# An order of work for 30 attention chunks: both score sets side by side, both transposes together, and routing in six parts

## The chip, the cores and the metric

The kernel runs on one core of one Trainium2 chip. The metric is the device time of one execution in microseconds (us), the median of several runs. Engines: TensorE (PE; PEld are its weight loads), VectorE (DVE), ScalarE (ACT), GpSimd (POOL), and SyncE (SP), which only issues DMAs.

## The reference

Sliding-window attention, and then a mixture of experts with one expert for each token:

```
scores = q @ k.T / 8 - slope_h * |i - j|     where 0 <= i - j < 128, else -1e9
attn   = softmax(scores);   x = (attn @ v), heads side by side   # 8 batches, 8 heads, 576 tokens, 64 wide
logits = x @ w_gate;        e = argmax(logits);   g = softmax(logits)[e]
out    = g * (relu(x @ w1[e]) @ w2[e])       # 4608 tokens, 512 wide, 8 experts, 1024 hidden
```

All inputs and the output are fp32.

## The kernel before, in words

The 4608 tokens are 36 chunks of 128 query rows. For a pair of batches there are nine chunks: four of the first batch, a "tail" chunk with the last 64 rows of both batches, and four of the second. The first chunk of a batch (m = 0) has no keys before it: its value products are 16 matmuls instead of 32, and nothing has to be masked. In a tail chunk they are 64 smaller ones. With chunk 0 first, the m = 0 chunks are 0, 5, 9, 14, 18, 23, 27 and 32, and the tail chunks 4, 13, 22 and 31.

A chunk goes through these operations, each of which exists for two sets of four heads (set 0 and set 1) where a digit follows the letter:

- S0, S1 (`scores`, lines 158 to 187; TensorE): 8 bf16 matmuls write the bias into a set's PSUM banks (L173), then 32 fp32 matmuls add q times k (L182), in array tiles of 64x32. There is one pair of banks for each set, so S0 of the next chunk needs the exponentials of set 0 of this chunk to be over, and S1 those of set 1.
- F0, F1 (`fold`; VectorE): a predicated copy puts the window's two halves into one (L192, left out for m = 0), and a maximum is taken (L195).
- E0a, E0b, E1a, E1b (`exps`; ScalarE): two heads each, exponential and sum (L224).
- T0, T1 (`turn`; TensorE): four 128x128 transposes into a PSUM bank (L232). C0, C1 (ScalarE) copy them into `pT` (L336). P0a to P1b (`select`; GpSimd) mask them (L247). Z (GpSimd) adds an epsilon to the sums.
- A0, A1 (`av`; TensorE): the value products (L263), in tiles of 128x64 into another bank of the same two-buffer pool that T0 and T1 use. X (ScalarE) copies them to `xT` (L345).
- R (`rows`; TensorE): 8 matmuls (128x128) turn `xT` back to rows and add the gate logits (L271), into the only buffer of `r_ps`. I, L, Y (VectorE): reciprocal of the sums, scaled logits and scaled rows (L276). Y also issues the DMA of the rows to memory on SP (L1308).

What stands where is written out by hand. Each operation has a time in chunks (the table `WHEN`, from line 402): operation "op" of chunk ch is issued at ch + WHEN[op], all operations are sorted by that, and each engine works through its own in that order. So in the table below T0=1.02 puts the first transposes of chunk ch just behind the first scores of chunk ch + 1:

```
WHEN = {None: dict(
    S0=0, F0=0.06, S1=0.063, E0a=0.332, E0b=0.407, F1=0.604, E1a=0.611, E1b=1.002, T0=1.02, C0=1.03,
    P0a=1.04, T1=1.043, P0b=1.282, C1=1.376, P1a=1.472, P1b=1.516, Z=1.753, A0=2.75, A1=2.76, X=2.963,
    I=3.06, R=4.027, L=4.119, Y=4.237)}
```

A quarter of a chunk is a step (`step`, line 355). Behind the operations of a step come the loads that fall due, the parts of `route` (L526 to L595: VectorE and a few bf16 matmuls that give each token its rank in its expert; a generator that runs to its next `yield` at every fourth step), and halves of the first expert's weights, which ScalarE rounds (`round_half`, L1078) and GpSimd subtracts (`rest_half`, L1083). Groups of five or six chunks are routed together (`GROUPS`); three late groups have steps of their own (`PACE`).

After the 36 chunks the order by hand ends (step 152), and the expert layers follow: TensorE multiplies in three passes of split precision (L767, L973), with rows gathered and scattered by GpSimd's indirect DMAs.

Of the kernel before, what the change touches and what calls it, by code (L numbers as in the profile page):

```python
# [36 lines left out]
def attention(ctx, tc, st, qT, qE, kT, v, c1, cb, iw, load_c2, logits, chunk_done, chunks, begun):  # L37
# [320 lines left out]
    def step(s):  # L358
        st["step"] = s
        if s == 0:  # L360
            begun(0)
        if s == 12:
            begun(1)
        for f in opening.get(s, ()):
            f()
        for f, b, m in ahead.get(s, ()):
            f(b, m)
        while plan and plan[0][0] < (s + 1) / 4 - 1e-6:
            _, _, op, ch = plan.pop(0)
            do(op, ch)  # L370
        if s < len(WU) - 1:
            warm_up(WU[s + 1])
        for k in list(st["stages"]):
            if k[1] <= s and (s in PACE[k[2]] if k[2] in PACE else s % 4 == STAGE):
                k[1] = s + 1
                if next(k[0], k) is k:
                    st["stages"].remove(k)
        n, i = divmod(s - FETCH, 8)
        for k in range(2):
            if 0 <= n < 7 and i == ROUND + 4 * k:  # L380
                st["round"](n, k)
            if 0 <= n - (REST + 4 * k) // 8 < 7 and i == (REST + 4 * k) % 8:
                st["rest_of"](n - (REST + 4 * k) // 8, k)
        n, i = divmod(s - FETCH + 12, 8)
        for k in range(2):
            if 0 <= n < 8 and i == LOAD + 4 * k:
                st["load"](n, k)
        if s in EP:
            early(EP[s])
        if s == HAND - 1:  # L390
            st["last"]()
# [6 lines left out]
    s = HAND  # L398
# [6 lines left out]
# [3 lines that stand above are left out]
# [1 line left out]
WHEN[1] = dict(T1=1.55, C1=1.56, P1a=1.57, P1b=1.58, U=1.61, Z=1.9)  # L409
WHEN[2] = dict(T1=1.057, C1=1.56, P1a=1.57, P1b=1.58, U=1.61, Z=1.9)  # L410
APIECE = (0, 1, 2)
WHEN[4] = dict(A0=2.26)
WHEN[13] = dict(A0=2.26)
WHEN[22] = dict(A0=2.26)
WHEN[31] = dict(A0=2.26)
WHEN[33] = dict(X=2.77, I=3.75, R=3.76, L=3.77, Y=3.78)
WHEN[34] = dict(A0=2.51, A1=2.52, X=2.53, I=3.25, R=3.26, L=3.27, Y=3.28)
WHEN[35] = dict(
    T0=1.02, C0=1.03, E1a=1.053, E1b=1.054, Z=1.055, T1=1.262, C1=1.31, P1a=1.32, P1b=1.456, A0=2.01,
    A1=2.02, X=2.03, I=2.55, R=2.56, L=2.57, Y=2.58)  # L420
STAGE = 3
ROUND = 0
REST = 7
# [13 lines left out]
FETCH = 57  # L437
# [80 lines left out]


def route(tc, st, lg, c0, G, groups):  # L520
    nc = tc.nc
    rp = st["rp"]
    run = st["run"]
# [26 lines left out]
        nc.tensor.matmul(out=rank[:, E * g:], lhsT=tri[:, 1, :], rhs=f2(oh[:, 0:G - g]), start=False, stop=g == G - 1)  # L550
    pick = rp.tile(sh3, F32, name="pick")
    nc.vector.tensor_tensor(out=pick, in0=rank.rearrange("p (g e) -> p g e", e=E), in1=oh, op=ALU.mult)
    gate = rp.tile([128, G], F32, name="gate")
    nc.vector.tensor_reduce(out=gate, in_=ex, axis=AX.X, op=ALU.add)
    put_gates(tc, st, gate, groups)
# [68 lines left out]
def route_last(tc, st, lg, ch, groups):  # L624
    nc = tc.nc
    rp = st["rp"]
    run = st["run"]
    tri = st["tri"]
    prev = rp.tile([128, E], BF16, name="l_prev", bufs=1)
    nc.vector.tensor_copy(out=prev, in_=run[:, ch, :])  # L630
    mx = rp.tile([128, 2], F32, name="l_mx", bufs=1)
    nc.vector.tensor_reduce(out=mx[:, 0:1], in_=lg, axis=AX.X, op=ALU.max)
    key = rp.tile([128, E], F32, name="l_key", bufs=1)
    nc.vector.scalar_tensor_tensor(out=key, in0=lg, scalar=mx[:, 0:1], in1=st["rev"], op0=ALU.is_ge, op1=ALU.mult)
    nc.vector.tensor_scalar(out=mx[:, 1:2], in0=mx[:, 0:1], scalar1=-1.0, scalar2=None, op0=ALU.mult)
    mk = st["mk"][:, ch:ch + 1]
    nc.vector.tensor_reduce(out=mk, in_=key, axis=AX.X, op=ALU.max)
    ex = rp.tile([128, E], F32, name="l_ex", bufs=1)
    gate = rp.tile([128, 1], F32, name="l_gate", bufs=1)
    nc.scalar.activation(out=ex, in_=lg, func=AF.Exp, bias=mx[:, 1:2], accum_out=gate)  # L640
    oh = rp.tile([128, E], BF16, name="l_oh", bufs=1)
    nc.vector.tensor_scalar(out=oh, in0=key, scalar1=mk, scalar2=None, op0=ALU.is_equal)
    rest = [r for r, *_ in st["stages"]]
    st["stages"].clear()
    st["warm"](0)
    rank = st["four"]()[:, 0, 0:E]
    nc.tensor.matmul(out=rank, lhsT=tri[:, 0, :], rhs=oh, start=True, stop=False)
    nc.tensor.matmul(out=rank, lhsT=tri[:, 1, :], rhs=prev, start=False, stop=True)
    for r in rest:
        next(r)  # L650
    put_gates(tc, st, gate, groups)
    for r in rest:
        next(r)
    rr = rp.tile([128, 2, E], BF16, name="l_rr", bufs=1)
    for k, n in enumerate(("tokh", "tokl")):
        nc.vector.tensor_scalar(out=rr[:, k, :], in0=oh, scalar1=st[n][:, ch:ch + 1], scalar2=None, op0=ALU.mult)
    pick = rp.tile([128, E + 56], F32, name="l_pick", bufs=1)[:, 0:E]
    s = st["rank"][:, ch:ch + 1]
    nc.vector.tensor_tensor_reduce(out=pick, in0=rank, in1=oh, op0=ALU.mult, op1=ALU.add, scale=1.0, scalar=0.0,
                                   accum_out=s)  # L660
    t0 = EARLY // 128
    lps = {}
    for t in range(t0, TT):
        lps[t] = rp.tile([128, 128], BF16, name=f"l_lp{t}", bufs=1)
        nc.vector.tensor_scalar(out=lps[t], in0=st["i128"], scalar1=s, scalar2=-128.0 * t, op0=ALU.subtract,
                                op1=ALU.is_equal)
    st["warm"](1)
    for r in rest:
        list(r)
    ip = st["four"]()[:, 0, 0:E * TT]  # L670
    for t, lp in lps.items():
        for k in range(2):
            nc.tensor.matmul(out=ip[:, E * t:E * t + E], lhsT=lp, rhs=rr[:, k, :], start=(k == 0), stop=(k == 1))
    st["warm"](2)
    v = lambda ap: ap.rearrange("p (e t) -> p t e", t=TT)
    nc.vector.tensor_tensor(out=v(st["idx"])[:, t0:], in0=v(st["base"])[:, t0:],
                            in1=ip.rearrange("p (t e) -> p t e", e=E)[:, t0:], op=ALU.add)
    nc.vector.tensor_copy(out=v(st["idx"])[:, 0:t0], in_=v(st["base"])[:, 0:t0])
    nc.vector.tensor_tensor(out=v(st["base"])[:, t0:], in0=v(st["base"])[:, t0:],
                            in1=ip.rearrange("p (t e) -> p t e", e=E)[:, t0:], op=ALU.add)  # L680
    nc.vector.tensor_tensor(out=run[:, ch + 1, :], in0=run[:, ch, :], in1=oh, op=ALU.add)
    for low in st["parts"][1:]:
        low()


# [91 lines left out]
def moe_early(ctx, tc, st):  # L777
# [8 lines left out]
    h = {}  # L786
    w = {}
    parts = []
    st["parts"] = parts

    def step(op, bank):
        if op == "z":
# [478 lines left out]
@with_exitstack  # L1271
def attn_moe_kernel(ctx, tc, qT, qE, kT, v, c1, cb, c2, iw, w12, out):
    nc = tc.nc
    st = {"stages": [], "w12": w12}
    moe_pools(ctx, tc, st)
    load_c2 = load_consts(tc, st, c2)
    moe_early(ctx, tc, st)
# [4 lines left out]
    with ExitStack() as actx:  # L1282
# [15 lines left out]
        def done(ch, subs, x_sb):  # L1298
            c0, G = next((c, n) for c, n in GROUPS if c <= ch < c + n)
            if ch == c0 + G - 1:  # L1300
                lg = lgp.tile([128, 8, E], F32, name="lg")[:, 0:G, :]
                nc.vector.tensor_reduce(out=lg, in_=lgs["all"].rearrange("q g p c e -> q g e (p c)"), axis=AX.X, op=ALU.add)
            for lo in (0, 2):
                if lo == 2 and subs[0][0] == subs[2][0]:
                    continue
                n = 64 if subs[0][0] != subs[2][0] else 128
                t0 = subs[lo][0] * S + QB * subs[lo][1]
                nc.sync.dma_start(out=st["xd"][t0:t0 + n].rearrange("t (p x) -> t p x", p=NP),  # L1308
                                  in_=x_sb[QB * lo:QB * lo + n])
            if ch == c0 + G - 1:  # L1310
                groups = []
                for k in range(G):
                    sb = chunks[c0 + k]
                    t0 = sb[0][0] * S + QB * sb[0][1]
                    if sb[0][0] != sb[2][0]:
                        groups.append((k, (0, 64, t0, 1)))
                        groups.append((k, (64, 64, sb[2][0] * S + QB * sb[2][1], 1)))
                    elif groups and groups[-1][1][1] == 128 and groups[-1][1][2] + 128 * groups[-1][1][3] == t0:
                        k0, (p0, n0, s0, m0) = groups[-1]
                        groups[-1] = (k0, (p0, n0, s0, m0 + 1))  # L1320
                    else:
                        groups.append((k, (0, 128, t0, 1)))
                if ch == N // 128 - 1:
                    st["last"] = lambda: route_last(tc, st, lg[:, 0, :], ch, groups)
                else:
                    r = route(tc, st, lg, c0, G, groups)
                    st["stages"].append([r, st["step"] + (c0 not in PACE), c0])

        attention(actx, tc, st, qT, qE, kT, v, c1, cb, iw, load_c2, logits, done, chunks, begun)
    st["rc"] = ctx.enter_context(tc.tile_pool(name="rc", bufs=1))  # L1330
# [44 lines left out]
```

## Time and profile before

| | us |
|---|---|
| median of 3 runs | 645.15 (645.06 to 647.49) |
| the profiled execution's own time | 640.79 |
| its span, first to last instruction | 639.1 |
| TensorE busy | 626.4 |
| VectorE busy | 385.2 |
| ScalarE busy | 315.4 |
| GpSimd busy | 295.0 |

An engine's busy time is what its instructions cover together. Matmuls overlap each other and their ends are modelled, so the distance from one group's start to the next group's start says more than their durations. A row of a timeline has the start, the time from first start to last end of a merged group, engine, line and operation, what is written and read, the tile in the array for matmuls, the shape, the count, and in brackets the idle time of the engine ahead of it with what ended it ("issue": nothing that the profile shows).

### The profile page before, as it was taken

Reading aid. Unit: us, or ns where it says so; the run is one execution under the profiler, and the core shown is the slowest. Engines: PE = TensorE matmul, PEld = TensorE weight load, DVE = VectorE, ACT = ScalarE, POOL = GpSimd, SP = SyncE. Lnnn points to the kernel's source line nnn. Section 1 sums busy time; section 2 is a strip of 40 time slices with the busy share of each in tenths; the row PEclk is TensorE's granted clock in tenths of the full one; section 3 lists DMA queues with packets and bytes.
Section 4 is the critical chain, followed back from the end, with each engine's and each line's share of the span. In section 5 each row is a group of like instructions: output and inputs, shape, how many; then the busy total and the mean of one; then the engine's idle time right before and its main releaser. Section 6 shows DMA issues by size and latency. Waiting matters only on the chain.

```text
span 639.1 us, 17958 instructions
## 1 busy us (share of the span) xinstructions
PE 626.4 (98%) x7125; PEld 540.9 (85%) x7125; DVE 385.2 (60%) x962; ACT 315.4 (49%) x939; POOL 295.0 (46%) x405
## 2 busy tenths in 40 slices
PE   8999999999999999999999999999999999999996
PEld 4778888888887988988989899899899998888884
DVE  5758877969888785536543664565465456356411
ACT  5878888888878314534342434334233333333311
POOL 3644657758646050067327606733760860580202
PEclk9999999999999999999999999999999999999998
DMA  8777887887743152474536425433543542544201
GB/s 247 218 233 190 281 246 224 233 251 214 225 131 87 51 185 70 160 251 112 187 115 169 108 75 183 121 91 127 158 108 100 172 117 88 181 120 136 68 1 61
DMA packets 60072, 97.44 MB, mean 152 GB/s; under 512 B 12293, under 2 KB 30597, under 8 KB 59986
## 3 DMA queue, kind: packets, MB, share of 16 engines
q1 hardware_dynamic: 51362, 76.25, 39.1%
q0 software_dynamic: 8336, 19.76, 11.4%
q8 instruction: 57, 0.93, 0.6%
q14 instruction: 29, 0.24, 0.1%
q10 hardware_dynamic: 288, 0.26, 0.1%
HBM read 77.27 MB, written 18.98 MB: 151 GB/s over the span
## 4 chain that ended last, share of the span: by engine, by line
PE 76%; issue 10%; DVE 6%; POOL 4%; ACT 3%; DMA 1%; POOLq 0%; ACTq 0%; DVEq 0%; SPq 0%
PE y_ps L973 25%; PE l_ps L767 25%; PE b_ps L263 7%; PE b_ps L232 4%; PE s_ps L182 4%; PE r_ps L271 4%; POOL xg L747 2%; PE s_ps L173 2%; ACT pe L224 2%; PE s_ps L767 1%; DVE s_ps L192 1%; DVE nmax L195 1%; POOL out L961 1%; DMA c_sb<-c 1%; PE x_ps L728 1%
## 5 line engine op out<-in xcount | busy, mean ns | idle before, releaser
L770 ACT ACTIVATE hh<-l_ps 128x320 fp32r<-128x320 f32 (+5 forms) x104 | 46.4, 448 | 198.2 <-PE l_ps L767 198.1
L774 DVE SCALAR_TENSOR_TENSOR hl<-l_ps,hh 128x320 fp32r<-128x320 f32 (+5 forms) x104 | 52.2, 502 | 145.6 <-ACT hh L770 145.5
L747 POOL DMA_INDIRECT xg<-xd,od_idx x112 | 116.8, 1043 | 34.5 <-issue 33.6
L224 ACT ACTIVATE pe<-s_ps,nmax 128x128 f32<-128x128 f32 x264 | 97.9, 390 | 27.2 <-DVE nmax L195 23.6
L973 PE MATMUL y_ps<-wh,hh 128*128 128x512 f32 x280 | 110.0, 393 | 0.0
L973 PE MATMUL y_ps<-wl,hh 128*128 128x512 f32 x280 | 109.5, 391 | 0.0
L973 PE MATMUL y_ps<-wh,hl 128*128 128x512 f32 x280 | 109.1, 390 | 0.0
L961 POOL DMA_INDIRECT out<-y,od_pidx x33 | 34.6, 1047 | 148.8 <-ACT y L979 142.7
L247 POOL TENSOR_SCALAR_AFFINE_SELECT pT<-pT 128x512 f32<-128x512 f32 x112 | 71.7, 648 | 59.6 <-ACT pT L336 56.4
L1066 DVE TENSOR_TENSOR wl<-w_raw,wh 128x512 fp32r<-128x512 f32 x114 | 73.8, 689 | 33.8 <-ACT wh L1062 32.2
L767 PE MATMUL l_ps<-xh,wh 128*128 128x320 f32 (+8 forms) x416 | 81.2, 317 | 0.0
L767 PE MATMUL l_ps<-xl,wh 128*128 128x320 f32 (+8 forms) x416 | 80.8, 316 | 0.0
L767 PE MATMUL l_ps<-xh,wl 128*128 128x320 f32 (+8 forms) x416 | 80.7, 316 | 0.0
L767 PEld LDWEIGHTS l_ps<-xh,wh 128*128 128x128 f32 x416 | 67.6, 188 | 6.7 <-issue 1.2
L767 PEld LDWEIGHTS l_ps<-xl,wh 128*128 128x128 f32 x416 | 66.1, 188 | 2.0
L767 PEld LDWEIGHTS l_ps<-xh,wl 128*128 128x128 f32 x416 | 65.9, 188 | 2.0
L263 PE MATMUL b_ps<-pT,v_sb 128*64 128x128 f32 (+2 forms) x1152 | 66.3, 265 | 0.8 <-issue 0.7
L263 PEld LDWEIGHTS b_ps<-pT,v_sb 128*64 128x64 f32 (+1 forms) x1152 | 57.1, 136 | 9.9 <-issue 5.2
L1062 ACT CAST wh<-w_raw 128x1024 fp32r<-128x1024 f32 x57 | 59.5, 1044 | 6.4 <-DMA w_raw<-w 6.4
L973 PEld LDWEIGHTS y_ps<-wh,hl 128*128 128x128 f32 x280 | 52.6, 188 | 11.4
L973 PEld LDWEIGHTS y_ps<-wh,hh 128*128 128x128 f32 x280 | 52.6, 188 | 9.9 <-ACT hh L770 0.4
L973 PEld LDWEIGHTS y_ps<-wl,hh 128*128 128x128 f32 x280 | 52.6, 188 | 9.2
(220 smaller groups left out, 935.1 us busy)
## 6 DMA issues: line engine op xcount, KB each, us to landing
w_raw<-w SPq DMA_DIRECT2D x56, 512.0 KB, 3.8
xd<-x_sb SPq DMA_DIRECT2D x32, 258.0 KB, 3.5
v_sb<-v SPq DMA_DIRECT2D x32, 256.0 KB, 4.6
q_sb<-qT SPq DMA_DIRECT2D x31, 256.0 KB, 4.4
k_sb<-kT SPq DMA_DIRECT2D x23, 256.0 KB, 5.4
w_raw<-w SPq DMA_DIRECT2D x16, 256.0 KB, 4.6
k_sb<-kT SPq DMA_DIRECT2D x8, 384.0 KB, 5.4
w_n<-w SPq DMA_DIRECT2D x3, 1024.0 KB, 5.4
```

What stands on the lines that cost most here:

```text
L182: nc.tensor.matmul(out=s_ps[rows(u), c, n, x0:x1], lhsT=blocks["q", b, m][h, 2 * g + n, rows(u % 2 if tail else u)], rhs=batch[b][h, 2 * g ...
L224: nc.scalar.activation(out=pe[:, h, :], in_=s_ps[:, c, n, lo:lo + 128], func=AF.Exp, bias=nmax[:, 2 * c + n:2 * c + n + 1], scale=1.0, acc ...
L247: nc.gpsimd.affine_select(out=part(cut(kb)), in_=part(cut(1)), pattern=pat(sign), base=0, channel_multiplier=-sign, compare_op=op, fill=0.0)
L263: nc.tensor.matmul(out=x_ps[64 * c:64 * c + 64, p, q], lhsT=blocks["v", b, m - 1 + kb][0:kk, D * h:D * h + D], rhs=pT[0:kk, kb, h, q], sta ...
L747: ins = tc.nc.gpsimd.indirect_dma_start(out=g[:, s], out_offset=None, in_=parts, in_offset=bass.IndirectOffsetOnAxis(ap=idx[:, s], axis=0),)
L767: nc.tensor.matmul(out=ps, lhsT=a[:, 128 * d:128 * d + 128], rhs=b[:, d], start=(k == 0), stop=(k == 11))
L770: nc.scalar.activation(out=hh, in_=ps, func=AF.Relu)
L774: nc.vector.scalar_tensor_tensor(out=hl, in0=ps, scalar=0.0, in1=hh.bitcast(F32), op0=ALU.max, op1=ALU.subtract)
L961: ins = nc.gpsimd.indirect_dma_start(**kw).ins
L973: nc.tensor.matmul(out=ys[t], lhsT=a[:, tl], rhs=b[:, 512:1024], start=(f == 0 and k == 0), stop=(f == 7 and k == 2))
L1062: keep(tc, nc.scalar.copy(out=wh, in_=raw))
L1066: keep(tc, eng.tensor_tensor(out=wl[:, sl], in0=raw[:, sl], in1=wh.bitcast(F32)[:, sl], op=ALU.subtract))
```

## The change

Chunks 5 to 34 get a table of their own. Both score sets stand at the head of a chunk, then both transposes of the chunk before, the row matmuls of the chunk three before (R at 3.41 instead of 4.027), and the value products of the chunk two before. Chunks 3 and 4 get the new times for R, I, L and Y, and chunk 4 an earlier E1b. The special A0 of tail chunks goes. Chunks 33 and 34 keep their own entries over the new table. `route` gets one more `yield` for the groups that have no steps of their own; its six parts run in turn at the third step of a chunk ("h") or, for the two with matmuls, at the fourth ("p"), at most one in a chunk. The rounding of weight halves comes one step earlier.

```diff
+        for k in list(st["parts"]):
+            if k[1] < s and s % 4 == (2, 3)[k[2][0] == "p"]:
+                k[1], k[2] = s + 1, k[2][1:]
+                if next(k[0], k) is k:
+                    st["parts"].remove(k)
+        n, i = divmod(s - FETCH + (s < 4 * SIDE[1]), 8)
         for k in range(2):
             if 0 <= n < 7 and i == ROUND + 4 * k:
                 st["round"](n, k)
+        n, i = divmod(s - FETCH, 8)
+        for k in range(2):
...
-WHEN[4] = dict(A0=2.26)
-WHEN[13] = dict(A0=2.26)
-WHEN[22] = dict(A0=2.26)
-WHEN[31] = dict(A0=2.26)
...
+SIDE = (5, 35)
+for ch in range(*SIDE):
+    WHEN[ch] = {**dict(
+        S0=0, S1=0.001, F0=0.16, T0=1.25, T1=1.33, C0=1.37, F1=0.38, R=3.41, E0a=0.46, P0a=1.5, E0b=0.55, P0b=1.6,
+        A0=2.61, I=3.62, L=3.63, Y=3.65, E1a=0.65, A1=2.75, E1b=0.8, C1=1.98, X=3.07, P1a=2.1, P1b=2.2, Z=1.3),
+        **(WHEN[ch] if ch > 32 else {})}
+for ch in (SIDE[0] - 2, SIDE[0] - 1):
+    WHEN.setdefault(ch, {}).update(R=3.41, I=3.62, L=3.63, Y=3.65)
+WHEN[SIDE[0] - 1].update(E1b=0.95)
+PARTS = "hphhhp"
...
     nc.vector.tensor_tensor(out=pick, in0=rank.rearrange("p (g e) -> p g e", e=E), in1=oh, op=ALU.mult)
+    if fine:
+        yield
     gate = rp.tile([128, G], F32, name="gate")
```

## Rows read from the trace of the kernel before

**Rows 1.** The page, part 1: busy us, share of the span and instructions of each engine.
```profile
PE 626.4 (98%) x7125; PEld 540.9 (85%) x7125; DVE 385.2 (60%) x962; ACT 315.4 (49%) x939; POOL 295.0 (46%) x405
```

**Rows 2.** Windows: length, then busy us (instructions) of each engine, clock, DMA share, GB/s.
```profile
27.52:196.28 168.76, 166.56 (x3949) 139.13 (x3948) 133.18 (x340) 141.39 (x590) 100.34 (x168) 1.00 0.75 219
...
223.00:639.00 416.00, 409.75 (x2312) 362.41 (x2309) 211.68 (x492) 142.04 (x242) 173.07 (x189) 1.00 0.42 125
```

**Rows 3.** Timeline of PE, a plain chunk (22), to the routing matmuls behind it.
```profile
122.64 0.33 PE L173 MATMUL s_ps<-cb_sb 64*32 64x320 bf16 x8
122.79 0.73 PE L182 MATMUL s_ps<-k_sb,q_sb 64*32 64x160 f32 x32
123.45 0.66 PE L232 MATMUL b_ps<-c_sb,pe 128*128 128x128 f32 x4
123.94 1.15 PE L271 MATMUL r_ps<-iw_sb,xT 128*128 128x144 f32 x8
124.92 0.60 PE L232 MATMUL b_ps<-c_sb,pe 128*128 128x128 f32 x4
125.45 0.33 PE L173 MATMUL s_ps<-cb_sb 64*32 64x320 bf16 x8
...
126.26 1.97 PE L263 MATMUL b_ps<-pT,v_sb 128*64 128x128 f32 x32
128.16 0.42 PE L593 MATMUL r_ps<-rr,lp 128*128 128x48 bf16 x10
```

**Rows 4.** Timeline of PE: routing matmuls straight before value products (chunk 31).
```profile
176.90 0.27 PE L550 MATMUL r_ps<-oh,tri 128*128 128x40 bf16 x5
177.10 1.97 PE L263 MATMUL b_ps<-pT,v_sb 128*64 128x128 f32 x32
```

**Rows 5.** Waits of PEld, 27.52 to 196.28: us in total, times, longest.
```profile
PEld b_ps L232 <- ACT pe L224: 1.3, 6, 0.2
```

**Rows 6.** Timeline of PE: groups that were held up (chunks 12, 21 and 24).
```profile
68.33 0.86 PE L232 MATMUL b_ps<-c_sb,pe 128*128 128x128 f32 x4
...
116.84 0.33 PE L173 MATMUL s_ps<-cb_sb 64*32 64x320 bf16 x8 [0.43 <-ACT pe L224]
116.97 1.04 PE L182 MATMUL s_ps<-k_sb,q_sb 64*32 64x160 f32 x32
...
139.28 1.61 PE L263 MATMUL b_ps<-pT,v_sb 64*64 64x64 f32 x38 [0.70 <-issue]
```

**Rows 7.** Timeline of ACT, chunk 22: an exponential, a copy, an exponential, a half-cast.
```profile
126.52 0.36 ACT L224 ACTIVATE pe<-s_ps,nmax 128x128 f32<-128x128 f32 x1
...
126.86 0.58 ACT L336 COPY pT<-b_ps 128x512 f32<-128x512 f32 x1
127.33 0.39 ACT L224 ACTIVATE pe<-s_ps,nmax 128x128 f32<-128x128 f32 x1
...
128.02 0.64 ACT L1078 CAST wh<-w_raw 128x512 fp32r<-128x512 f32 x1
```

**Rows 8.** Timeline of DVE: a fold, and a routing part up to the next fold.
```profile
121.02 0.70 DVE L192 COPY_PREDICATED s_ps<-c_sb,s_ps 128x512 f32<-128x512 uint32 x1 [0.38 <-PE s_ps L182]
121.75 0.69 DVE L195 TENSOR_REDUCE nmax<-s_ps 128x4 f32<-128x512 f32 x1
122.36 0.47 DVE L580 TENSOR_TENSOR c<-c,t 128x5 f32<-128x5 f32 x1
...
124.92 0.41 DVE L192 COPY_PREDICATED s_ps<-c_sb,s_ps 128x256 f32<-128x256 uint32 x1
```

**Rows 9.** Timeline, chunks 4 and 5: an exponential on ACT, the logits on DVE.
```profile
28.34 0.39 ACT L224 ACTIVATE pe<-s_ps,nmax 128x128 f32<-128x128 f32 x1
...
29.88 0.23 DVE L276 TENSOR_TENSOR lg_all<-r_ps,rinv 128x64 f32<-128x64 f32 x1 [0.70 <-PE r_ps L271]
```

**Rows 10.** Timeline of PE: transposes of chunk 35, value products of chunk 34.
```profile
204.20 1.21 PE L232 MATMUL b_ps<-c_sb,pe 128*128 128x128 f32 x4
205.34 1.97 PE L263 MATMUL b_ps<-pT,v_sb 128*64 128x128 f32 x32
```

More of the change, by code (lines that the diff above doesn't have):

```diff
@@ L377, in step @@
                     st["stages"].remove(k)
-        n, i = divmod(s - FETCH, 8)
+        for k in list(st["parts"]):
[4 more added lines that the diff above has]
+        n, i = divmod(s - FETCH + (s < 4 * SIDE[1]), 8)
         for k in range(2):
@@ L520, in route @@
 def route(tc, st, lg, c0, G, groups):
+    fine = c0 not in PACE
     nc = tc.nc
@@ L681, in route_last @@
     nc.vector.tensor_tensor(out=run[:, ch + 1, :], in0=run[:, ch, :], in1=oh, op=ALU.add)
-    for low in st["parts"][1:]:
+    for low in st["low_parts"][1:]:
         low()
@@ L788, in moe_early @@
     parts = []
-    st["parts"] = parts
+    st["low_parts"] = parts
     def step(op, bank):
@@ L1273, in attn_moe_kernel @@
     nc = tc.nc
-    st = {"stages": [], "w12": w12}
+    st = {"stages": [], "parts": [], "w12": w12}
     moe_pools(ctx, tc, st)
@@ L1326, in done @@
                     r = route(tc, st, lg, c0, G, groups)
-                    st["stages"].append([r, st["step"] + (c0 not in PACE), c0])
+                    if c0 in PACE:
+                        st["stages"].append([r, st["step"], c0])
+                    else:
+                        st["parts"].append([r, st["step"], PARTS])
         attention(actx, tc, st, qT, qE, kT, v, c1, cb, iw, load_c2, logits, done, chunks, begun)
```

## The prediction

> **What bounds the kernel now.** I read the page's busy shares first: TensorE is at 98% [rows 1]. Then the windows: the stretch from chunk 5's first score matmul (27.52) to chunk 35's (196.28) holds the 30 chunks that are reordered. It takes 168.76 us, 5.63 per chunk, with the clock granted in full; TensorE is busy for 166.56 of it, ScalarE for 141.39, VectorE for 133.18 [rows 2]. The expert stage behind it, from 223 us on, is TensorE's too, so time saved or lost ahead of it reaches the end. Third, TensorE's timeline of a plain chunk. The ends of matmuls are modelled, so I go by starts: scores to transposes 0.81, four transposes 0.49, row matmuls 0.98, four transposes and the way to the next scores 0.53, scores to value products 0.81, value products 1.90, in all 5.52 [rows 3]. So the chunk is bound by TensorE's own work and by the gaps where it changes kind; waits for other engines are the rest of the 5.63.
>
> The waits have places. The last transpose of the second set waits for the last exponential, six times [rows 5]; such a group takes 0.86 [rows 6] where a plain one takes 0.60 [rows 3]: about 0.26 each, 1.5 with one longer. In chunk 21 routing on VectorE makes the folds late: the gap ahead of the scores is 0.43 and the scores take 1.04 [rows 6] for 0.73 [rows 3], 0.8 in all. Smaller waits of this sort, read off the same timeline, add 0.8. Together 3.1 us could go. Two more gaps, "issue" inside a run of equal matmuls (0.70 in [rows 6], another at 40.3), are no wait for an engine; I keep them on both sides.
>
> **The change part by part.** *Order on TensorE.* The kinds ran scores, transposes, rows, transposes, scores, values; now scores twice, transposes twice, rows, values. The 32 score matmuls go in four waves: from first start to last end 0.73, one takes 0.30, so waves are (0.73-0.30)/3 = 0.145 apart, and a second score block can follow 0.15+0.43+0.145 = 0.73 after the first began, where transposes follow after 0.81 [rows 3]: 0.08 saved. The gap from transposes to scores (0.53 against 4 x 0.11 = 0.44) goes, but one from row matmuls to value products comes. No row shows fp32 row matmuls followed by value products. Bounds: 0.20 from start to start, as from transposes to scores, which cancels exactly; or 0.10 less, since routing's last bf16 matmul group to value products takes only 177.10-176.90 = 0.20 for all five matmuls [rows 4], which would save 3 us more over 30 chunks. I take the cancelling end, since the nearer row has fp32 operands of the same size. Sum: 30 x -0.08 = -2.4 (from -5.4 to 0).
>
> What the second gap is: when the kind changes, the weight loads of the new kind start late, and only then. The Trainium skill, TensorEngine Tiling (Array Packing), section Key Properties, says that changing the tiling mode drains the engine; by it the step from 128x128 row matmuls to 128x64 value products pays like the others, which speaks against the larger saving; the routing row by itself would allow it.
>
> *ScalarE's ring.* The second score set of the next chunk may not overwrite its banks before this chunk's last exponential. From the second scores' start: 0.81 to the transposes, 0.65 to their modelled end, about 0.1 to the copy, copy 0.47, eight exponentials of 0.35, 0.2 until the last result is in and seen [rows 3, 7]: 5.0 us. A plain chunk leaves 5.44, so 0.4 is to spare. In the seven chunks whose value products are 16 instead of 32 (7, 11, 16, 20, 25, 29, 34), TensorE wants only 5.44-0.88 = 4.56, and waits 0.45. Routing matmuls in two of these fill 0.6: 7 x 0.45 - 0.6 = +2.5 (from 0 to +4). The old waits of 3.1 go, since their place goes: the last transpose now has a whole block of scores before it.
>
> The x copy, the half-cast of weights (0.64, one step earlier) and the second pT copy run on ScalarE before the transposes end: after the last exponential there is about 1.6 us until the first pT copy can start, and the three need 0.47+0.47+0.5. Cost nothing; without that cover each would lengthen the ring by its own time.
>
> *VectorE.* Folds take 1.34 each [rows 8]; two folds, reciprocal, logits and rows end 4.9 us into a chunk, and the next fold is due at 6.5. A routing part has some 1.6 us, and late folds are hidden by another 0.2 behind the copy and the ring's 0.4. The largest part (clipped position, one-hot, two products) took 122.36 to 124.92, 2.56 [rows 8]: over by some 0.3 at worst. The first part's exponential stands between two score exponentials and waits for VectorE: 0.35 where the ring has no room, once. I take +0.4 (from 0 to +5: sixteen VectorE parts by 0.3).
>
> *GpSimd and SP.* The second set's selects now follow the copy at the next chunk's head, ahead of a weight half and the first set's selects; the value products are two thirds of a chunk behind: nothing. The row writes wait on SP in the third quarter instead of the first; behind them stand loads of v for two chunks later: nothing. Without that distance a late load would show as waiting value products.
>
> *The seam.* Chunk 4 has the old order for its copies and exponentials, chunk 5 the new one. (i) Chunk 4's last exponentials started at 28.34 [rows 9]; they move ahead of one copy (0.47) to 27.87 and end near 28.7. The second score set of chunk 5 is now due at 27.52+0.62 = 28.14: +0.6. (ii) On VectorE the logits of an older chunk (order 5.119) now stand before chunk 5's first fold (5.16). They waited for the row matmuls already [rows 9]; now the fold waits behind them, about 2 us later, exponentials end late, and chunk 6's scores wait 0.3 and 0.7: +1.0. (iii) In chunk 6 two row groups fall together (order 6.027 and 6.41) on one PSUM buffer. Logits, first fold (1.34) and rows (0.7) of the first stand between: the second starts 1.8 late, and TensorE is in order. Sum +3.4 (from +1 to +4.5). The second row group itself (0.98) is work drawn forward.
>
> *The end.* Chunk 36 has no row matmuls of chunk 32 any more (-0.98). The last transposes of chunk 35 waited before too: 1.21 for 0.60, value products at 205.34 [rows 10], 9.06 after chunk 35's first score matmul. Now a pT copy stands before its last exponentials: x copy until 6.1, copy 6.6, four exponentials 8.1, products at 8.5. So -0.6, the moved rows included.
>
> Sum: -2.4 -3.1 +2.5 +0.4 +3.4 +1.0 (rows drawn forward) -0.6 = +1.2. The profiled execution took 640.79 (span 639.1 and 1.7 around it) and would become 642.0; the median of the runs shown is 4.4 above it, so I carry the difference over: 645.15 + 1.2 = 646.3 us.
>
> **Rivals.** (1) Faster: the ring and the seam are paid from slack. For: ScalarE is idle for 16% of the stretch [rows 2] and it waited, not worked, ahead of many exponentials. Against: the order is fixed on each engine, and the seam's orders are read directly. Then -2.4 -3.1 and the end's gain: about -5, 640.0. (2) Slower: VectorE. Routing now falls in six parts between the row scaling and the next fold, a hole of 1.6 us. If VectorE reaches that hole half a microsecond later than I reckon, because the row matmuls now come behind both transposes, the fold is late in each chunk with a routing part, and the ring's room is used up: sixteen parts by 0.3 to 0.5 add 5 to 8 to my sum: about 652. It decides where parts exceed 1.6+0.6 us; for it speaks the 2.56, against it that the other parts are near 1.5. (3) The row-to-value gap is cheap, as the bf16 row: another -3, 643. (4) The order on TensorE is not what ends these chunks, other waits fill what is freed: no change, 645.
>
> **Chances.** Forecast 0.47 (its own range 643.5 to 649), rivals 0.15, 0.17, 0.10, 0.11. A measurement of this kernel can tell about 0.5%, 3.2 us, from no change. Faster: rival 1 and a third of rival 3 with its neighbours, 0.20. Slower: rival 2 and the upper edge of the forecast, 0.23. Same: 0.57. The range 640.5 to 650 leaves out part of rival 1 and most of rival 2, about 2 in 10, and holds the ends of the costs added with mixed signs.
>
> **What would show it.** Right: in the timeline after, transposes start 0.73+0.81 after the first scores; row matmuls to value products near 1.07; a plain chunk near 5.44; gaps of 0.45 before the second scores in the chunk after a 16-product one, released by an exponential; 1.8 us before the second row group of chunk 6. Wrong: no gap there (rival 1); idle TensorE before scores, released by VectorE, in the routing chunks (rival 2); 0.98 from rows to values (rival 3). A new wait on a load of v or q, or "issue" gaps inside the doubled score block, would be a cost that I have not counted.

## The result, and the profile after

Over 13 runs each the changed kernel takes 648.63 us (646.88 to 650.58), the kernel before 644.62 (642.68 to 647.49): ratio 1.0063 [1.0049, 1.0077], 4.0 us slower. The forecast was +1.2 us, 646.3 within 640.5 to 650. So the time lies inside the range, and 0.63% (0.49 to 0.77) stands at the edge of the 0.5% which can be told from no change: a little slower, where no difference was given the larger chance. Forecast and measurement differ by 2.8 us, and several terms were off in both directions; the largest single miss, 2.0 us, is the end of the attention stage.

The profiled execution of the changed kernel took 647.77, span 646.0. The new lines shift those behind line 377 (`step` stands at line 358 in both kernels, the table `WHEN` at 404 before and 411 after): the transposes and bias matmuls keep L232 and L173, the rank matmuls are L560 now, the last routing matmuls L609, the first expert layer L783.

The page after, part 1 (busy us, share of the span, instructions of each engine), to stand beside [rows 1]:

```profile
PE 625.3 (97%) x7123; PEld 545.8 (84%) x7125; DVE 384.6 (60%) x962; ACT 313.1 (48%) x939; POOL 294.9 (46%) x405
```

Windows after (length, then busy us of each engine, clock, DMA share, GB/s), from chunk 5's first scores to chunk 35's, and from 223 us on, to stand beside [rows 2]:

```profile
27.26:198.19 170.93, 164.78 (x3960) 144.52 (x3959) 134.42 (x341) 140.42 (x596) 101.97 (x169) 1.00 0.73 218
...
223.00:646.00 423.00, 414.46 (x2347) 365.67 (x2345) 214.31 (x510) 143.72 (x249) 172.09 (x189) 1.00 0.39 123
```

TensorE is busy 1.8 us less in the reordered stretch, and the stretch is 2.2 us longer: 6.15 us without work, where it had 2.20. The clock is granted in full both times.

TensorE's timeline after, a plain chunk (19), to stand beside [rows 3]:

```profile
108.01 0.33 PE L173 MATMUL s_ps<-cb_sb 64*32 64x320 bf16 x8
108.15 0.73 PE L182 MATMUL s_ps<-k_sb,q_sb 64*32 64x160 f32 x32
108.70 0.32 PE L173 MATMUL s_ps<-cb_sb 64*32 64x320 bf16 x8
108.83 0.82 PE L182 MATMUL s_ps<-k_sb,q_sb 64*32 64x160 f32 x32
109.58 1.09 PE L232 MATMUL b_ps<-c_sb,pe 128*128 128x128 f32 x8
110.51 1.15 PE L271 MATMUL r_ps<-iw_sb,xT 128*128 128x144 f32 x8
111.59 1.97 PE L263 MATMUL b_ps<-pT,v_sb 128*64 128x128 f32 x32
113.49 0.19 PE L560 MATMUL r_ps<-oh,tri 128*128 128x40 bf16 x1
```

From the first scores to what follows the value products it is 113.49 - 108.01 = 5.48, where it was 5.52. Row matmuls to value products are 111.59 - 110.51 = 1.08, as forecast (1.07): the new change of kind costs what the old one did. The first score block gives way after 0.69, as forecast up to 0.04; but the second runs 0.82 where the first runs 0.73, so 0.04 is saved in a chunk and not 0.08.

TensorE's timeline after, the groups that were held up; in brackets the idle time and what ended it. Chunk 5's second scores, chunk 6's two score sets and its second row group, the second scores of chunks 8 and 21, and the routing matmuls that end chunks 29, 33 and 34:

```profile
28.46 0.30 PE L173 MATMUL s_ps<-cb_sb 64*32 64x256 bf16 x8 [0.45 <-ACT pe L224]
...
33.58 0.33 PE L173 MATMUL s_ps<-cb_sb 64*32 64x320 bf16 x8 [0.19 <-ACT pe L224]
...
34.98 0.33 PE L173 MATMUL s_ps<-cb_sb 64*32 64x320 bf16 x8 [0.50 <-ACT pe L224]
...
39.36 1.22 PE L271 MATMUL r_ps<-iw_sb,xT 128*128 128x144 f32 x8 [1.46 <-DVE x_sb L276]
...
47.57 0.33 PE L173 MATMUL s_ps<-cb_sb 64*32 64x320 bf16 x8
...
48.75 0.33 PE L173 MATMUL s_ps<-cb_sb 64*32 64x320 bf16 x8 [0.31 <-ACT pe L224]
...
119.48 0.33 PE L173 MATMUL s_ps<-cb_sb 64*32 64x320 bf16 x8 [0.29 <-ACT pe L224]
...
168.06 0.46 PE L609 MATMUL r_ps<-rr,lp 128*128 128x48 bf16 x12 [0.52 <-DVE x_sb L276]
...
192.46 0.46 PE L609 MATMUL r_ps<-rr,lp 128*128 128x48 bf16 x12 [1.14 <-DVE x_sb L276]
...
198.01 0.17 PE L560 MATMUL r_ps<-oh,tri 128*128 128x24 bf16 x1 [0.49 <-DVE x_sb L276]
```

The waits down to 119.48 (and their like in chunks 12 and 17) are the forecast's seam and ring, in its places and close to its sizes. The bracket counts from the modelled end of the matmuls before; from start to start the second scores of chunk 8 come 48.75 - 47.57 = 1.18 after the first, where 0.69 is normal: 0.49, against 0.45 forecast. The last three were not forecast.

TensorE's timeline after, chunk 35, to stand beside [rows 10]:

```profile
198.18 0.33 PE L173 MATMUL s_ps<-cb_sb 64*32 64x320 bf16 x8
...
202.95 1.97 PE L263 MATMUL b_ps<-pT,v_sb 128*64 128x128 f32 x32 [1.12 <-ACT pT L336]
205.59 0.66 PE L232 MATMUL b_ps<-c_sb,pe 128*128 128x128 f32 x4 [0.68 <-ACT xT L345]
...
207.34 1.38 PE L232 MATMUL b_ps<-c_sb,pe 128*128 128x128 f32 x4 [0.66 <-ACT pe L224]
208.65 2.20 PE L263 MATMUL b_ps<-pT,v_sb 128*64 128x128 f32 x32
```

The value products of chunk 34 start 10.47 after chunk 35's first scores; it was 9.06, and 8.5 was forecast. Three waits in a row, each released by ScalarE.

By the starts of a chunk's first scores, the changed kernel is 0.27 ahead at chunk 5 (27.25 against 27.52), 4.11 behind at chunk 7 (42.97 against 38.86), 0.06 behind at chunk 29 (162.87 against 162.81) and 1.90 behind at chunk 35 (198.18 against 196.28). The first matmul of the second expert layer is 3.55 behind (226.45 against 222.90). 2.0 us of what is regained between belongs to this one execution of the kernel before: its "issue" gaps at 40.3 and at 139.28 [rows 6], which the changed kernel does not show. Counted from start to start, the score matmuls of chunk 7 take 1.69 to the transposes where 0.66 is normal, and the 64 value products in chunk 24 take 3.42 where those in chunk 33 take 2.46. Without these gaps the stretch from chunk 5 to chunk 35 costs 1.90 + 0.27 + 2.0 = 4.2 us. In a second profile of the changed kernel (e8) the stretch is 0.56 shorter, which makes 3.6.

Behind the first matmul of the second expert layer the profiles differ by another 3.3 us, of which at least 2.6 are no part of the change. Waits after from 223 us on (us in total, times, longest):

```profile
PEld l_ps L783 <- issue: 2.9, 6, 1.2
PE l_ps L783 <- issue: 1.3, 2, 0.9
```

They stand in the expert layers, which the change does not touch, and the two rows are largely the same gaps, seen at the weight loads and at the matmuls. The kernel before has 1.2 and none there, and e8's profile of the changed kernel has the same 1.2 and none. From start to start, three groups of four matmuls take 3.62 in the first profile (287.18 to 290.80) where e8's take 1.77, and another gap costs 0.46 at 363.88: 2.3 of the 2.6 us by which the first profile is longer than e8's from that matmul on.

### The profile page after: what moved, and what is told of

It is laid out like the page before. It is cut to its first block, busy times and chain, and to the rows that moved or that the text cites. A ratio compares the mean times of both kernels' runs of the same rounds, so it can differ in the third digit from the quotient of the medians.

```text
span 646.0 us, 17928 instructions
## 1 busy us (share of the span) xinstructions
PE 625.3 (97%) x7123; PEld 545.8 (84%) x7125; DVE 384.6 (60%) x962; ACT 313.1 (48%) x939; POOL 294.9 (46%) x405
## 4 chain that ended last, share of the span: by engine, by line
PE 79%; issue 9%; DVE 6%; ACT 4%; POOL 2%; POOLq 0%; ACTq 0%; DVEq 0%
PE y_ps L989 27%; PE l_ps L783 26%; PE b_ps L263 7%; PE s_ps L182 5%; PE b_ps L232 4%; PE r_ps L271 4%; ACT pe L224 3%; PE s_ps L173 2%; PE s_ps L783 1%; POOL out L977 1%; DVE s_ps L192 1%; DVE nmax L195 1%; POOL xg L763 1%; DVE x_sb L276 1%; PE x_ps L744 1%
## 5 line engine op out<-in xcount | busy, mean ns | idle before, releaser
L224 ACT ACTIVATE pe<-s_ps,nmax 128x128 f32<-128x128 f32 x264 | 93.5, 383 | 7.1 <-DVE nmax L195 6.6
L783 PE MATMUL l_ps<-xl,wh 128*128 128x320 f32 (+8 forms) x416 | 81.0, 316 | 1.3 <-issue 1.3
L783 PE MATMUL l_ps<-xh,wh 128*128 128x320 f32 (+8 forms) x416 | 81.4, 317 | 0.0
L783 PE MATMUL l_ps<-xh,wl 128*128 128x320 f32 (+8 forms) x416 | 80.7, 316 | 0.0
L783 PEld LDWEIGHTS l_ps<-xh,wh 128*128 128x128 f32 x416 | 67.5, 188 | 7.2 <-issue 1.2
L783 PEld LDWEIGHTS l_ps<-xl,wh 128*128 128x128 f32 x416 | 66.1, 188 | 3.7 <-issue 1.7
L783 PEld LDWEIGHTS l_ps<-xh,wl 128*128 128x128 f32 x416 | 65.9, 188 | 2.0
```

The lines of the kernel that those rows point to most:

```text
L224: nc.scalar.activation(out=pe[:, h, :], in_=s_ps[:, c, n, lo:lo + 128], func=AF.Exp, bias=nmax[:, 2 * c + n:2 * c + n + 1], scale=1.0, acc ...
L783: nc.tensor.matmul(out=ps, lhsT=a[:, 128 * d:128 * d + 128], rhs=b[:, d], start=(k == 0), stop=(k == 11))
```

## The experiments

Two theories stood at the start. A: the losses lie in separate places (the near seam, ScalarE's ring, the routing matmuls at chunk ends, the far end), each with a cause of its own in the written order, and what one of them gives back reaches the end. B: they are paid from one slack, so that another wait takes the place of one that is removed. Each group of runs has its own runs of the kernel before on the same chip: 640.66 us for e1 to e4, 640.96 for e5 to e8, 641.14 for e9 to e11.

**e1, the near seam.** First folds of chunks 5 and 6 ahead of the logits on VectorE:

```diff
+for ch in (5, 6):
+    WHEN[ch].update(F0=0.1)
```

> The changed kernel, with the first folds of chunks 5 and 6 ahead of the logits of the older chunk on VectorE (F0 at 0.1 instead of 0.16). Theory A (the loss sits in the seams): the waits before chunk 6's scores (0.25 and 0.68) go and the second row group of chunk 6 waits under 0.4 instead of 1.6; the start of chunk 7 comes about 2.3 us earlier against the changed kernel, and it stays so to the end: 646.3 on the median. Theory B (the new order itself is what costs; ScalarE and VectorE are too full, and what is freed at one place is waited for at the next): chunk 7 starts earlier, but the lead is gone by chunk 12, and the end is within 0.5 us of the changed kernel's 648.6.

643.99 us, ratio 1.0051 [1.0034, 1.0069]. From the start of the last transpose to the second row group of chunk 6 it is 0.41 instead of 1.73. From chunk 5 to chunk 7 the kernel gains 1.5 us on the first profile of the changed kernel (1.2 on e8's), and to chunk 35 the gain is 1.7 (1.1): it is kept, as A had it, but it is smaller than the 2.3 that A expected, and in time it is 0.8 us, with intervals that overlap the changed kernel's. The two score sets of chunk 6 wait as before, so VectorE's order was not their cause. The timeline of e1, ScalarE's and TensorE's rows, shows it:

```profile
32.56 0.59 ACT L336 COPY pT<-b_ps 128x512 f32<-128x512 f32 x1 [0.78 <-PE b_ps L232]
33.05 0.37 ACT L224 ACTIVATE pe<-s_ps,nmax 128x128 f32<-128x128 f32 x1
...
34.43 0.39 ACT L224 ACTIVATE pe<-s_ps,nmax 128x128 f32<-128x128 f32 x1
34.61 0.33 PE L173 MATMUL s_ps<-cb_sb 64*32 64x320 bf16 x8 [0.19 <-ACT pe L224]
```

Chunk 4's second copy to pT, still at its old place, stands ahead of chunk 5's exponentials and waits for transposes that the old order issues behind the row matmuls. The exponentials queue behind that wait.

**e2, the far end.** Chunk 34's second copy earlier, chunk 35's first exponentials behind chunk 34's first copy:

```diff
-WHEN[34] = dict(A0=2.51, ...
+WHEN[34] = dict(C1=1.7, A0=2.51, ...
-    T0=1.02, C0=1.03, E1a=1.053, E1b=1.054, ...
+    T0=1.02, C0=1.03, E0a=0.38, E1a=0.72, E1b=0.74, ...
```

> The changed kernel, with ScalarE's order mended around chunk 35: chunk 35's exponentials behind the first pT copy of chunk 34 (E0a at 0.38) and its second set's ahead of the xT copy of chunk 33 (E1a, E1b at 0.72, 0.74), the second pT copy of chunk 34 at 35.70. Theory A: value products of chunk 33 no longer wait 1.1 for a pT copy, transposes of chunk 35 no longer 0.7 and 0.7 plus 0.7; value products of chunk 34 start about 7.3 after chunk 35's first scores instead of 10.47, and 2 to 3 us of it reach the end: 646.1. Theory B: the chain through the last chunk's routing and the gathers sets the start of the expert layers, not TensorE: under 0.7 us reaches the end.

643.18 us, 1.0031 [1.0018, 1.0044]: 2.0 us of the 4 come back. TensorE's timeline of e2, chunk 35's first scores and the value products of chunk 33 and, in three rows, of chunk 34:

```profile
197.70 0.33 PE L173 MATMUL s_ps<-cb_sb 64*32 64x320 bf16 x8
...
201.28 1.97 PE L263 MATMUL b_ps<-pT,v_sb 128*64 128x128 f32 x32
...
205.47 1.09 PE L263 MATMUL b_ps<-pT,v_sb 128*64 128x128 f32 x16
206.82 0.44 PE L263 MATMUL b_ps<-pT,v_sb 128*64 128x128 f32 x4 [0.26 <-POOL pT L247]
207.54 0.88 PE L263 MATMUL b_ps<-pT,v_sb 128*64 128x128 f32 x12 [0.27 <-POOL pT L247]
```

Chunk 34's now start 7.77 after the scores (10.47 in the changed kernel), and the value products of chunk 33 wait for nothing. Of the 2.7 us gained there, part is lost at once, since the value products of chunk 34 now wait twice for GpSimd's selects: the row matmuls behind them start 11.14 after chunk 35's first scores, where it was 13.09 in the changed kernel. That is 2.0 less, as in the timed runs. ScalarE's timeline of the changed kernel shows what was taken away:

```profile
201.52 0.37 ACT L224 ACTIVATE pe<-s_ps,nmax 128x128 f32<-128x128 f32 x1 [1.91 <-DVE nmax L195]
...
202.22 0.58 ACT L336 COPY pT<-b_ps 128x512 f32<-128x512 f32 x1
```

The first exponentials of chunk 35 kept their old time, 0.332, the first copy of chunk 34 moved to 0.37: the copy now stands behind exponentials that wait 1.91 for a fold, which VectorE does behind a routing part. The bank that this copy frees is the one that the value products of chunk 33 want.

**e3, the late routing groups.** The group from chunk 21 on gets other steps:

```diff
-PACE = {21: (122, 126, 130, 132, 135), ...
+PACE = {21: (119, 122, 126, 130, 135), ...
```

> The changed kernel, with the parts of the routing of chunks 21 to 26 at steps 119, 122, 126, 130, 135 instead of 122, 126, 130, 132, 135, so that none falls between the two folds of chunk 33. Theory A: the routing matmuls at the end of chunk 33 no longer wait 1.1 us for the row scaling; chunk 34 starts 1.0 us earlier against chunk 33 and so does the end: 647.6. Theory B: VectorE has the same work and the wait shows up one or two chunks earlier: end within 0.4 us of 648.6.

645.26 us, 1.0058 [1.0037, 1.008], not to be told from the changed kernel: the wait at the end of chunk 33 is gone, but rank matmuls at 175.31 wait 1.40 for the row scaling instead. B's answer for this place.

**e4, ScalarE's ring.** Second scores later in the six chunks behind a 16-product one:

```diff
+for ch in (8, 12, 17, 21, 26, 30):
+    WHEN[ch].update(S1=0.34)
```

> The changed kernel, with the second score set behind both transposes (S1 at 0.34) in chunks 8, 12, 17, 21, 26 and 30, those after a chunk with 16 value products. Theory A (ScalarE's ring from second scores to second scores is longer than such a chunk): the four waits of 0.5 before the second scores of chunks 8, 12, 17, 21 are gone; two more changes of kind cost about 0.2 per chunk, so 4 x 0.3 - 2 x 0.2: 0.8 us less, 647.8. Theory B (the gap is there because the two score blocks stand together, such as weight loads or instruction supply, whatever ScalarE does): the gap before these second scores stays 0.3 or more or shows in the chunk behind: no gain.

650.77 us, 1.0154 [1.0123, 1.0184], slower by another 0.9%. Timeline of e4, chunk 8, TensorE and ScalarE:

```profile
47.90 0.41 ACT L224 ACTIVATE pe<-s_ps,nmax 128x128 f32<-128x128 f32 x1
48.24 0.63 ACT L336 COPY pT<-b_ps 128x512 f32<-128x512 f32 x1
48.92 1.14 PE L232 MATMUL b_ps<-c_sb,pe 128*128 128x128 f32 x8 [0.78 <-ACT pT L336]
```

The transposes need the bank which that copy frees, and ScalarE does it behind its eight exponentials. So the ring is a sequence of ScalarE's, and the later place of the second scores did not avoid it. The loss itself stood in neither theory: A had 0.8 us of gain, B no gain.

**e5 and e11, routing alone; e6, the order alone; e8, the changed kernel again.** e5 is the kernel before with the six parts of `route` and their steps, the old table and the old rounding step. e6 is the changed kernel with the old five parts:

```diff
-    fine = c0 not in PACE
+    fine = False
...
-                    if c0 in PACE:
-                        st["stages"].append([r, st["step"], c0])
-                    else:
-                        st["parts"].append([r, st["step"], PARTS])
+                    st["stages"].append([r, st["step"] + (c0 not in PACE), c0])
```

> The kernel before, with the change's routing alone: six parts in the order hphhhp at the third and fourth step of a chunk, the old table of times and the old rounding step. Theory A (seams and ScalarE's chain cost, routing in parts helps): late folds in chunks 18 to 21 go, about 1 us faster than the kernel before, ratio 0.9985. Theory C (the six parts are themselves the cost, since they put routing between row scaling and next fold on VectorE): slower than before by 1 us or more, with new gaps ahead of score or routing matmuls, released by VectorE.

> The changed kernel, with routing as before (five parts, all at the fourth step of a chunk). Theory A: the seams, ScalarE's chain and the far end stay, 4 us over the kernel before, and routing parts at the chunk's end, right ahead of the next fold, add waits of 0.5 in some ten chunks: ratio 1.008 to 1.011. Theory C: without the six parts the loss is gone, ratio 1.000 to 1.003.

> The changed kernel itself once more, on the chip of the other runs of this call: ratio 1.0063 as before within 0.0015, and a second profile that tells which of its gaps come back: those at chunks 6, 8, 12, 17, 21, 29, 33 and from chunk 35 on should be there to within 0.1 us; the gaps in the expert layers that end on issue (2.9 us in the first profile) should not.

e5: 639.06 us, 0.9963 [0.9946, 0.998]. e6: 648.07, 1.0103 [1.0083, 1.0123]. e8: 645.49, 1.0065 [1.0044, 1.0086]. The order alone costs 1%, and the routing seems to give some of it back (the intervals of e6 and e8 just touch). In e5 the gap of 0.43 ahead of chunk 21's first scores [rows 6] is gone:

```profile
113.73 0.93 PE L263 MATMUL b_ps<-pT,v_sb 128*64 128x128 f32 x13
114.59 0.33 PE L173 MATMUL s_ps<-cb_sb 64*32 64x320 bf16 x8
114.74 1.02 PE L182 MATMUL s_ps<-k_sb,q_sb 64*32 64x160 f32 x32
```

The long scores behind it (1.04 before, 1.02 here) stay, so the forecast counted them to that wait wrongly. The waits at chunks 6, 8, 12, 17, 21 and 33 and from chunk 34's end on return in e8's profile to within 0.1 us. The one at the end of chunk 29 does not (0.29 for 0.52), and e8 has one of 0.33 in chunk 27, for GpSimd's Z, which the first profile lacks. The "issue" gaps of the expert layers don't return.

> The kernel before with routing in six parts and nothing else, as in e5. If what e5 showed holds, 0.9963 again within 0.002, and faster than e10 by 0.2 to 0.4%. If e5 was chance, a ratio near 1.

e11, the same kernel as e5: 639.95 us, 0.9987 [0.9967, 1.0007]. The two intervals overlap between 0.9967 and 0.998. Routing alone has the lowest ratios of all versions that were run, 0.1 to 0.4% below the kernel before. That is less than the 0.5% that can be told from no change, and e11's interval holds 1: a gain is likely and not shown.

**e7, several mended together.** The edits of e1 and e2, chunk 4's second copy and selects at the new times, and one routing step moved:

```diff
-WHEN[SIDE[0] - 1].update(E1b=0.95)
+WHEN[SIDE[0] - 1].update(E1b=0.95, C1=1.98, P1a=2.1, P1b=2.2)
...
-PACE = {21: (122, 126, 130, 132, 135), ...
+PACE = {21: (122, 126, 130, 131, 135), ...
```

> The changed kernel with three places mended: at the near seam, first folds ahead of the older logits in chunks 5 and 6 and the second pT copy of chunk 4 behind chunk 5's exponentials (C1 at 1.98, its selects at 2.1 and 2.2); around chunk 35 as in the tail experiment; and the fourth routing part of chunks 21 to 26 at step 131 instead of 132, no longer between the folds of chunk 33. Theory A: near seam 1.6 + 0.9 less, far end 2 less, chunk 33 0.6 less: 5 us less than the changed kernel, 0 to 1 us under the kernel before, ratio 0.998 to 1.001. Theory B (each wait that is removed comes back in the next chunks): at most 2.5 us less than the changed kernel, ratio over 1.003.

642.71 us, 1.0027 [1.0008, 1.0046]: 2.4 us less than e8, where A expected 5 and B at most 2.5, so B's number came nearer. With chunk 4's copy and selects moved beside e1's edit, both score sets of chunk 6 start without a wait that the profile names, and chunk 7 starts 13.24 after chunk 5 where e1 has 14.25: that settles what e1 left open. The step at 131 made its place worse: the routing matmuls wait 1.55 at the end of chunk 33, where they waited 1.14.

**e9, the routing matmuls behind the scores.** They go from a chunk's end to behind both score sets of the next chunk, and the early gather (L822), which needs them, one step later:

```diff
-            if k[1] < s and s % 4 == (2, 3)[k[2][0] == "p"]:
+            p = k[2][0] == "p"
+            if k[1] < s - 2 * p and s % 4 == 2 - 2 * p:
...
+PACE = {21: (122, 126, 130, 132, 136), 27: (136, 140, 143, 146, 148), 30: (149, 150)}
+EP = {..., 136: "g", ...
```

> The changed kernel with the routing parts that hold matmuls issued behind both score sets of the next chunk, instead of at the chunk's end; two steps of the late groups and the early gather go with them. Theory A: at a chunk's end these matmuls wait because VectorE still reads their buffer (row scaling); behind two score sets (1.2 us) it is done. The gaps of 0.5, 1.15 and 0.5 at the ends of chunks 30, 33 and 34 go, and 1 to 2.1 us of them stay gone: ratio near 1.004. Theory B (those waits only stand where the ScalarE ring would wait anyway): gaps of the same size show up before the second scores or the transposes of the next chunk, and the ratio stays at 1.006.

("Chunk 30" there is the end of chunk 29.) 644.18 us, 1.0048 [1.0031, 1.0065], 1.1 us better than e8, though the intervals overlap. TensorE's timeline of e9, the second scores of chunks 30, 34 and 35:

```profile
169.20 0.33 PE L173 MATMUL s_ps<-cb_sb 64*32 64x320 bf16 x8 [0.34 <-ACT pe L224]
...
193.25 0.33 PE L173 MATMUL s_ps<-cb_sb 64*32 64x320 bf16 x8 [0.86 <-ACT pe L224]
...
198.79 0.33 PE L173 MATMUL s_ps<-cb_sb 64*32 64x320 bf16 x8 [0.53 <-ACT pe L224]
```

No routing matmul waits at a chunk's end any more, and in all three places a wait for an exponential has come in its stead. Behind the 16-product chunks 29 and 34 the second scores come 1.21 and 1.41 after the first, where 0.69 is normal: that is the ring, which the routing matmuls had hidden, and moving them gained 0.2 us at most up to chunk 33. (In chunk 26 it shows too now, 1.18.) The gain lies at chunk 33, which is no 16-product chunk: from its first scores to chunk 35's it is 11.89, where it was 12.96 in the changed kernel and 12.95 in e8, although chunk 34's second scores now wait 0.86 for exponentials, which ScalarE starts late because it waits 1.41 for chunk 33's second fold. From chunk 29 to chunk 35 the kernel now loses 0.53 against the one before, where the changed kernel lost 1.84 (1.60 in e8). So both theories hold in part: about 1.1 us were the routing matmuls' own, and two of the three waits covered the ring.

**e10, e9 with e7's two ends.**

> The kernel of e9 and with it the mended near seam and far end of e7. Theory A (the four losses lie in different places and add): 1.0065 less 0.0045 for seam and end less 0.002 to 0.003 for the routing matmuls, ratio 0.999 to 1.001, with the ScalarE ring (4 x 0.48) as what is left. Theory B: no better than e7, 1.0027.

641.21 us, 1.0009 [0.999, 1.0028], in the range that A gave, with B's 1.0027 at the upper edge of the interval: losses in different places add, as far as this can tell. It can't be told from the kernel before: the ring (0.17 to 0.54 idle in seven places) and the late part in chunk 33 (0.85) are still paid.

## Why the prediction was right in place and short in size

| term | forecast, us | measured, us, and from what |
|---|---|---|
| order on TensorE | -2.4 | -1.2: 30 x (5.48 - 5.52), worked out from one plain chunk of each |
| old waits | -3.1 | not measured by themselves |
| ScalarE's ring | +2.5 | +2.9: 4 x 0.48, and 0.5 at each of two chunk ends, where e9 shows the ring behind the wait |
| routing parts on VectorE | +0.4 | the six parts against five, on the old order: -0.8 and -2.4 (e11, e5) |
| seam, with rows drawn forward | +4.4 | +4.38, lag from chunk 5 to chunk 7 (4.09 in e8) |
| wait at the end of chunk 33 | none | +1.15 |
| end | -0.6 | +1.4 (10.47 - 9.06) |

- *The bound.* TensorE's starts set the chunk, as the forecast read them; the second change of kind costs what the first did, so rival 3 is out by a row (1.08, where it wanted 0.98). The Trainium skill, TensorEngine Tiling (Array Packing), section Key Properties, says that a change of tiling mode drains the engine; the row agrees in so far as this change of kind costs as much as the others, and it shows no draining as such. The bf16 routing group of [rows 4] was no guide for fp32.
- *Order.* The mechanism was right and the size half: the second score block, straight behind the first, runs 0.09 longer in the trace. The waves of 0.145 were read off a block that stands alone. Why the second runs longer stays open.
- *Ring.* Right in mechanism, in place and in size. Where routing matmuls stand at a chunk's end (29 and 34), they waited in its place, and the trace then names VectorE; only e9 showed ScalarE behind them.
- *Seam.* Its sum was right, and one of its causes wrong. (i) and (iii) are as forecast (chunk 5's second scores 28.46 - 27.25 = 1.21 behind the first, where 0.62 was reckoned without the wait: 0.59 against 0.6; and 1.73 against 1.8). (ii) was put down to the logits ahead of the first fold; e1 undid that, and the gaps stayed; e7 moved chunk 4's second copy, and they went. That (ii) came out near its +1.0 (e7 gains 1.01 on e1 up to chunk 7) was luck, since the forecast worked it out from another wait.
- *VectorE.* Rival 2 looked for folds late in each of sixteen routing chunks. The groups without steps of their own show none of that. Where VectorE costs most is one place: in chunk 33 a part of a late group stands between the two folds.
- *The end, the step that failed.* The forecast summed ScalarE's order as x copy until 6.1, one pT copy until 6.6, four exponentials until 8.1, products at 8.5. Two things in this sum were wrong. It took chunk 34's first copy to be free to run once its transposes were over; but that copy moved to 0.37, the first exponentials of chunk 35 stayed at 0.332 ahead of it, and these waited 1.91 for a fold behind a routing part. That makes the value products of chunk 33 late by 1.1, and the x copy behind them. And two pT copies stand between the x copy and the last exponentials, chunk 34's second and chunk 35's first, which waits for the transposes behind the x copy:

```profile
204.95 0.59 ACT L345 COPY xT<-b_ps 128x512 f32<-128x512 f32 x1 [1.44 <-PE b_ps L263]
205.44 0.59 ACT L336 COPY pT<-b_ps 128x512 f32<-128x512 f32 x1
206.34 0.59 ACT L336 COPY pT<-b_ps 128x512 f32<-128x512 f32 x1 [0.31 <-PE b_ps L232]
206.82 0.37 ACT L224 ACTIVATE pe<-s_ps,nmax 128x128 f32<-128x128 f32 x1
```

From chunk 35's first scores (198.18) the x copy gives way after 7.26 instead of 6.1, and the exponentials start after 8.64 instead of 6.6: of the 2.0 us, 1.2 are the late x copy and 0.9 the second pT copy. e2 changed both orders at once, and 2.0 us reached the end of the kernel. This accounts for the end coming out at +1.4 instead of -0.6; how much each of the two gives back by itself was not run.

VectorE's timeline of the changed kernel, chunk 33, shows the other missed wait:

```profile
187.72 0.69 DVE L195 TENSOR_REDUCE nmax<-s_ps 128x4 f32<-128x512 f32 x1
...
188.72 0.46 DVE L599 TENSOR_TENSOR eq<-c_sb,c 128x288 f32<-128x288 f32 x1
189.21 0.83 DVE L603 TENSOR_TENSOR rr<-eq,c_sb 128x288 bf16<-128x288 f32 x2
189.96 0.69 DVE L192 COPY_PREDICATED s_ps<-c_sb,s_ps 128x512 f32<-128x512 uint32 x1
...
191.72 0.68 DVE L276 TENSOR_TENSOR x_sb<-r_ps,rinv 128x512 f32<-128x512 f32 x1
```

The two folds of a chunk follow each other in the new table, but the late group's step (132) was left where it stood, and its part now separates them by 1.6 us. The second fold, the row scaling behind it and the routing matmuls, which wait for the scaling to leave their buffer, are all late by that.

Up to chunk 35 the terms that were measured by themselves make -1.2 + 2.9 + 4.38 + 1.15 = +7.2, and the stretch costs 4.2, so the old waits and the routing parts together must have brought some -3.0; -2.7 was forecast. How these two share it stays open: e6 against e8 gives 1.0103 against 1.0065 for the six parts in the new order, some 2.4 us, but their intervals just touch. With the end's 1.4 the stretch makes 5.6, where the timed runs say 4.0 [3.2, 5.0]. By e8's profile of the changed kernel it is 5.0, the edge of that interval; the rest stays open, since there is one profile of the kernel before.

## What to carry to other kernels

When an order is written out by hand, read it at its edges: where old and new entries meet, list each engine's queue by the new times, and ask of every instruction that waits what stands behind it; here both ends together cost what the middle could not bring. A wait that a profile names at one engine may cover another behind it: move the waiting instruction, and see which wait takes its place before its whole length is counted as a gain. And of a change in several parts, run each part alone: here the order cost 1%, and the part beside it, run alone, cost nothing and may have gained a little.

## What the runs showed of the hardware

- The second of two equal blocks of 32 score matmuls, straight behind the first, ran 0.82 from first start to last end, and the first 0.73, in the plain chunks.
- "Issue" gaps of 0.3 to 0.9 us inside runs of equal matmuls come and go from one execution to the next: in one profile of the changed kernel they cost 2.3 us in the expert layers, counted from start to start, in the other none stood there; the profile of the kernel before has two in the attention stage, 2.0 us. Two profiles of kernels that differ by 4 us can't be subtracted without taking these out first.
